# Two joint stretches of small tiles a batch: the next batch's maxima and shifts earlier, the softmax of 96 tokens later, the copies inside the stretch

## The chip, the cores and the metric

One Trainium2 chip, one core of it. The metric is the device time of one execution in microseconds (us); lower is better. The core's engines run side by side, each through its own instructions in order: TensorE (PE) multiplies matrices, VectorE (DVE), ScalarE (ACT) and GpSimd (POOL) work on tiles, and SyncE (SP) starts the transfers (DMA). An instruction waits on semaphores for what it needs, and everything behind it on its engine waits with it.

## The reference

For each of 8 batches and 8 heads (576 tokens, 64 channels, 32 memory slots), and then one feed-forward network over all tokens:

```python
a = exp(phi - max over tokens); a = a / (sum over tokens + 1e-9)
k_m, v_m = a^T k, a^T v                          # 32 slots a head
scores = q k_m^T / 8                             # 32 scores a token
attn = softmax(scores); x = attn v_m             # heads side by side: 512 channels
h = x @ w_in                                     # 512 -> 2048
g = where(h > 0, h, exp(min(h, 0)) - 1)
out = g @ w_out                                  # 2048 -> 512
```

## The kernel before

All matrix products of the network are made three times over: each operand is split into a high part (rounded by an ACT copy) and a low part (what a DVE subtraction leaves), and the products high by high, low by high and high by low are summed. `vw` (the slots' values times `w_in`) is small, so x is never formed: `hidden` multiplies the probabilities `A` by `vw`.

A batch's main loop has 32 iterations, numbered on through the batches: first half of the tokens (288) with 16 blocks j of 128 hidden channels, then the second half. Iteration `it` is a chain over the engines: `hidden(it)` on PE (L812, 6 matmuls into a `psh` bank, of which there are two), `elu_exp` on ACT (L827, L828), `elu_max` and `elu_rest` on DVE (L839, L847), `elu_high` on ACT (L859), `elu_low` on DVE (L865), and `project(it)` on PE (L873, 6 matmuls into two `pso` banks that gather a half's output). Of a half's 288 tokens 256 go through `project`; the last 32 are kept in `rest`, and after every second batch `rest_project` takes them together (48 matmuls more).

What a batch needs before its loop is made while the previous batch's loop runs:

- summaries: `load_phi`, `phi_max` (DVE, L442: the maximum over tokens, `nm`), `spread_max` (two DMAs on SP: L278 writes `nm` to DRAM as `nmd`, L281 reads it back into all rows as `nmb`), `load_e`, `e_shift` (POOL, L286: adds `nmb` to a second copy `e` of phi that lies by token), `e_exp` (ACT, L290), `phi_exp` (ACT, L447, gives the sums), `slot_scale`, and `slots` (PE, L493: the sums k_m and v_m)
- scores: 192 tokens are one score group `u`; `turn` (DVE, L641) transposes it, `softmax_max`, `softmax_shift`, `softmax_exp`, `softmax_sum`, `softmax_divide` (L654, L675, L679, L685 to L688, L696) and `turn_back` (L718) follow, and `probs_high`, `probs_low` (L740, L754) split the result into `A`
- `vw` for four blocks `c` of 512 hidden channels (L566), with `vw_high` (ACT, L768) and `vw_low` (DVE, L774).

Small tiles on PE (`vw`, scores, `slots`: 64 rows by 32 columns) stand together in two stretches a batch from batch 3 on. The first, 10.1 iterations before the batch's loop, holds `vw` of c = 1 and 0 and the scores of two groups; the second, 2.9 iterations into it, holds `vw` of c = 2 and 3, the next batch's `slots` and the third score group.

The order is a hand-written list `FIRST` up to the start of batch 2's loop, and from there a plan: `at(place, step)` gives each step a number in iterations (`base` is the batch's first iteration), the steps are sorted by it, and each engine gets its instructions in that order. SP's queue gets its transfers in the same order. By rule `hidden(it)` has place it - 1.7, `elu_high` it - 1, `project` it + 0.6; an `it` in the set `behind` has its `hidden` at it - 1.35, which puts a `project` between a stretch and it. Banks are named by letters: w, x, y, z are the four `pso` banks, h the two `psh`, b the two `psb`. Tiles of 2 KB a row come from one pool of seven buffers (`t2k`).

Of the kernel before, what the change touches and what calls it, by code (L numbers as in the profile page):

```python
# [8 lines left out]
F32 = mybir.dt.float32  # L9
# [165 lines left out]
def fused_kernel(ctx: ExitStack, tc: tile.TileContext, phiT, phi, kv0, kvt, kv, kvb, q0, q1, w_in, w_out, out):  # L175
# [64 lines left out]
    def units(b):  # L240

        if b < NB:
            return (0, HALF), (HALF, S)
        return (0, 192), (192, 384), (384, 576)
# [29 lines left out]
    def spread_max(b):  # L274

        s = st[b]
        d = dram.tile([2, P], F32, name="nmd")
        nc.sync.dma_start(d.rearrange("a x -> x a"), s["nm"])  # L278
        s["nmb"] = work.tile([P, 2 * P], F32, name="nmb", bufs=1)[:, :P]
        for a in range(2):  # L280
            nc.sync.dma_start(s["nmb"][64 * a : 64 * a + 64], d[a].partition_broadcast(64))  # L281
# [153 lines left out]
    def phi_max(b, g=None):  # L435
# [6 lines left out]
        eng.tensor_reduce(s["nm"][:, g], s["ph"][:, g], AX.X, ALU.max, negate=True)  # L442

# [167 lines left out]
    def scores_part(b, u, outs):  # L611
        by_head(outs, st[b]["kvm"][:, 0], st[b]["q"][u])
        st[b]["ps"]["s", u] = outs

    def scores_first(b):
        ps = [bank([P, 2, UT], "b") for _ in range(2)]
# [3 lines left out]
    def next_slots(b):  # L620
# [3 lines left out]
        if b + 1 == B:  # L624
            return
# [6 lines left out]
    def scores_last(b):  # L632
        scores_part(b, 2, [x[:, :UT] for x in st[b].pop("both")])

    def turn(b, u):

        s = st[b]
        n = s["q"][u].shape[-1]
        sc = temp(b, "sc", u, 2 * n)
        for a, ps in enumerate(s["ps"].pop(("s", u))):  # L640
            nc.vector.transpose(sc[:, a * n : (a + 1) * n], ps)  # L641
        s["sc"][u] = sc.rearrange("p (n m) -> p n m", m=SQ)

    def softmax_max(b, u):
# [6 lines left out]
        else:  # L651
            sc = st[b]["sc"][u]
            mx = mx[:, : sc.shape[1]]
# [3 lines left out]
    def softmax_shift(b, u):  # L657
# [15 lines left out]
        n = sc.shape[1]  # L673
        eng = nc.gpsimd if (b, u) in shift_on_pool else nc.vector
        eng.tensor_tensor(sc, sc, mx.unsqueeze(2).to_broadcast([P, n, SQ]), ALU.subtract)  # L675
# [5 lines left out]
    def softmax_sum(b, u):  # L681
        sc = st[b]["sc"][u]
        n = sc.shape[1]
        sm = work.tile([P, 2 * HALF // SQ], F32, name="sm")[:, :n]
        nc.vector.tensor_reduce(sm, sc, AX.X, ALU.add)  # L685
        nc.vector.tensor_scalar(sm, sm, EPS, None, ALU.add)
        rs = work.tile([P, 2 * HALF // SQ], F32, name="rs")[:, :n]
# [331 lines left out]
    def summaries(b, o, phi_at, max_at, e_at, kv_at, exp_at, shift_at, e_exp_at):  # L1019
        at(o + phi_at, load_phi, b)  # L1020
# [130 lines left out]
```

## Time and profile before

| | |
|---|---|
| median of 3 runs | 728.88 us (728.75 to 730.68) |
| the profiled execution's own time, and its span | 732.18 us, 730.3 us |
| PE busy in the span | 700.3 us (96%) |
| DVE, ACT, POOL busy | 458.2, 455.8, 66.3 us (63%, 62%, 9%) |
| mean granted TensorE clock | 0.992 of full speed |

The span is what the trace covers; the time has 1.9 us more around it. The profiled execution was 3.3 us (0.45%) above the median, so terms are summed against its own time and the result is then carried to the median. A busy PE in this profile is not PE at its peak: matmuls that begin late can be shown as busy.

### The profile page before, as it was taken

The page shows a single profiled execution, that of the slowest core. Times are in us where ns is not written, and L with a number is a line of the kernel's source. Part 1 is how long each engine was busy: PE and PEld are TensorE (multiplying, and loading weights), DVE is VectorE, ACT ScalarE, POOL GpSimd, SP SyncE. Part 2 cuts the span into 40 slices and gives each one's busy share as a digit, 9 for nine tenths or more (in the row PEclk, how much of TensorE's full clock was granted, in tenths as well). Part 3 has the DMA queues.
Part 4 walks back from the last instruction along what each step waited for, and adds up shares of the span by engine and source line. Part 5 has one row for each costly group of instructions (what it writes and reads, how often), then busy time and mean ns, then how long its engine had stood idle before and what let it go on. Part 6 is the DMA issues. An engine that isn't in the chain of part 4 may idle for free.

```text
span 730.3 us, 14339 instructions
## 1 busy us (share of the span) xinstructions
PE 700.3 (96%) x5496; PEld 582.3 (80%) x5496; DVE 458.2 (63%) x1207; ACT 455.8 (62%) x1101; POOL 66.3 (9%) x111
## 2 busy tenths in 40 slices
PE   7899999997999998999989999899989999999997
PEld 7778888886878877788867888678878787878886
DVE  3989888974586358464663646755584554856442
ACT  2879988875357556666653665656565555656652
POOL 0322342122000101000000000100010000000000
PEclk9999999999999999999999999999999999999999
DMA  9972023330302514201222011310141200000001
GB/s 345 408 310 87 2 90 109 115 121 19 131 34 77 198 62 167 83 13 62 75 92 78 32 62 43 154 66 1 62 167 37 73 1 30 1 30 0 30 1 44
DMA packets 25780, 64.14 MB, mean 88 GB/s; under 512 B 4848, under 2 KB 6384, under 8 KB 25712
## 3 DMA queue, kind: packets, MB, share of 16 engines
q1 hardware_dynamic: 25040, 63.06, 24.1%
q8 instruction: 44, 0.72, 0.4%
q10 hardware_dynamic: 672, 0.16, 0.1%
q14 instruction: 24, 0.20, 0.1%
HBM read 53.77 MB, written 9.44 MB: 87 GB/s over the span
## 4 chain that ended last, share of the span: by engine, by line
PE 75%; DVE 11%; ACT 5%; DMA 5%; issue 3%; POOL 1%; SPq 0%; POOLq 0%; DVEq 0%; ACTq 0%
PE pso L873 44%; PE psh L812 22%; DMA nmd<-nm 2%; PE psb L493 2%; DVE gf L839 2%; PE psb L566 2%; PE pso L566 2%; DVE vw L774 2%; ACT gf L828 1%; PE psh L566 1%; DMA nmb<-nmd 1%; ACT gf L827 1%; ACT gp L859 1%; DVE gp L865 1%; DMA kvt<-kv 1%
## 5 line engine op out<-in xcount | busy, mean ns | idle before, releaser
L873 PE MATMUL pso<-wout,gp 128*128 128x512 f32 x1728 | 441.7, 395 | 13.2 <-DVE gp L865 8.7
L873 PEld LDWEIGHTS pso<-wout,gp 128*128 128x128 f32 x1728 | 310.9, 189 | 75.7 <-DVE gp L865 11.1
L812 PEld LDWEIGHTS psh<-A,vw 128*128 128x128 f32 x1536 | 226.2, 188 | 37.1 <-issue 5.5
L812 PE MATMUL psh<-A,vw 128*128 128x288 f32 x1536 | 245.3, 297 | 7.0 <-DVE vw L774 3.4
L859 ACT CAST gp<-gf 128x256 fp32r<-128x256 f32 x256 | 103.3, 405 | 94.2 <-DVE gf L839 83.2
L827 ACT ACTIVATE gf<-psh 128x288 f32<-128x288 f32 x256 | 104.4, 408 | 84.0 <-PE psh L812 79.8
L865 DVE TENSOR_TENSOR gp<-gf,gp 128x256 fp32r<-128x256 f32 x256 | 112.3, 441 | 67.4 <-ACT gp L859 67.0
L839 DVE SCALAR_TENSOR_TENSOR gf<-gf,psh 128x256 f32<-128x256 f32 x192 | 80.1, 417 | 114.3 <-ACT gf L828 112.2
L828 ACT ACTIVATE gf<-gf 128x288 f32<-128x288 f32 x256 | 113.9, 445 | 8.1
L286 POOL TENSOR_TENSOR e<-e,nmb 128x512 f32<-128x512 f32 (+1 forms) x18 | 19.1, 1082 | 334.7 <-DMA e<-phi 155.4
L836 DVE SCALAR_TENSOR_TENSOR gf<-gf,psh 128x288 f32<-128x288 f32 x64 | 28.5, 450 | 17.5 <-ACT gf L828 16.3
L847 DVE SCALAR_TENSOR_TENSOR rest<-gf,psh 128x32 f32<-128x32 f32 x192 | 34.5, 180 | 0.0
L774 DVE TENSOR_TENSOR vw<-psh,vw 128x512 fp32r<-128x512 f32 x20 | 12.9, 686 | 24.4 <-ACT vw L768 24.4
L917 ACT CAST gp<-rest 128x256 fp32r<-128x256 f32 x32 | 12.6, 405 | 21.9 <-PE pso L873 21.9
L768 ACT CAST vw<-psh 128x512 fp32r<-128x512 f32 x20 | 10.8, 589 | 23.8 <-PE psh L566 23.8
L855 POOL COPY rest<-gf 128x32 f32<-128x32 f32 x64 | 18.6, 317 | 71.3 <-DVE gf L836 71.3
L922 DVE TENSOR_TENSOR gp<-rest,gp 128x256 fp32r<-128x256 f32 x32 | 12.9, 420 | 15.6 <-ACT gp L917 15.6
L388 ACT ACTIVATE mag<-raw 128x512 uint32<-128x512 uint32 x30 | 20.1, 672 | 2.7 <-DVE win L410 1.4
L384 ACT ACTIVATE mag<-raw 128x512 f32<-128x512 f32 x30 | 19.6, 666 | 0.0
L774 DVE TENSOR_TENSOR vw<-pso,vw 128x512 fp32r<-128x512 f32 (+1 forms) x28 | 17.4, 629 | 2.5 <-ACT vw L768 2.0
L493 PEld LDWEIGHTS psb<-kvt,e 64*32 64x32 f32 x864 | 13.6, 111 | 3.4 <-issue 3.3
L970 PE MATMUL pso<-ident 128*128 128x128 f32 x84 | 13.6, 325 | 1.6 <-POOL ident masks.py:199 1.6
(137 smaller groups left out, 482.1 us busy)
## 6 DMA issues: line engine op xcount, KB each, us to landing
kvt<-kvb SPq DMA_DIRECT2D x24, 512.0 KB, 6.4
raw<-w_in SPq DMA_DIRECT2D x15, 512.0 KB, 8.0
raw<-w_out SPq DMA_DIRECT2D x15, 512.0 KB, 8.2
out<-osb SPq DMA_DIRECT2D x14, 512.0 KB, 2.8
qt<-q SPq DMA_DIRECT2D x18, 384.0 KB, 4.5
kvt<-kv SPq DMA_DIRECT2D x8, 512.0 KB, 9.5
ph<-phiT SPq DMA_DIRECT2D x7, 576.0 KB, 5.0
e<-phi SPq DMA_DIRECT2D x12, 256.0 KB, 4.6
```

What stands on the lines that cost most here:

```text
L493: nc.tensor.matmul(ps[a][32 * j : 32 * j + 32], e[r, 32 * j : 32 * j + 32], t[r, k % 2, :, j], start=(k == 0), stop=(k == NBL - 1), tile_p ...
L566: nc.tensor.matmul(outs[a][32 * j : 32 * j + 32, :], lhs[r, 32 * j : 32 * j + 32], rhs[r, j], start=True, stop=True, tile_position=(64 * a ...
L774: nc.vector.tensor_tensor(t[:, LO, a, n0:n1], s["ps"]["vw", c, n0][a], t[:, HI, a, n0:n1], ALU.subtract)
L812: nc.tensor.matmul(ps, t[:, x, g, c0 : c0 + P], s["A"][hf][:, y, g, :], start=(n == 0), stop=(n == 5),)
L827: nc.scalar.activation(gf, ps, AF.Relu, scale=-1.0)
L828: nc.scalar.activation(gf, gf, AF.Exp, scale=-1.0)
L836: nc.vector.scalar_tensor_tensor(gf, gf, -1.0, ps, ALU.add, ALU.max)
L839: nc.vector.scalar_tensor_tensor(gf[:, :n], gf[:, :n], -1.0, ps[:, :n], ALU.add, ALU.max)
L847: nc.vector.scalar_tensor_tensor(rest_of(b, j)[:, o : o + REST], gf[:, n:], -1.0, ps[:, n:], ALU.add, ALU.max)
L859: nc.scalar.copy(gp[:, HI], gs[it][:, : NT * P])
L865: eng.tensor_tensor(gp[:, LO], gf[:, : NT * P], gp[:, HI], ALU.subtract)
L873: nc.tensor.matmul(ps, gp[:, y], wout[j][:, x, :], start=(first and n == 0), stop=(last and n == 2),)
```

## The change

`spread_max` no longer writes 256 single numbers: `phi_max` now also copies the two maxima of each row 16 times over into a 32-column tile (L453) and transposes that in 32 by 32 blocks on DVE (L454), so that 8 rows hold 32 numbers each, and the write to DRAM (L282) takes these 8 rows. This holds for batches 2 to 7. Places of the summaries move: `load_phi` from -14 to -21, `phi_max` from -11.3 to -18, `load_e` from -8.5 to -17, `phi_exp` from -6.45 to -16.2, `e_shift` from -5 to -14, `e_exp` from -3.3 to -13 (all against the running batch's base). The second score group of batches 3 to 7 is cut into two softmax units of 96 tokens, and the one that belongs to the second half of the tokens is worked on after the loop's start. In the first stretch `vw` of c = 1 and the scores change banks, and all four copies of a stretch's two `vw` blocks stand directly behind it. `base + 5` joins `behind`. The last batch's second stretch has another order.

```diff
     def spread_max(b):
 
         s = st[b]
-        d = dram.tile([2, P], F32, name="nmd")
-        nc.sync.dma_start(d.rearrange("a x -> x a"), s["nm"])
-        s["nmb"] = work.tile([P, 2 * P], F32, name="nmb", bufs=1)[:, :P]
+        t = s["nmb"]
+        nT = t[:, P + SQ : P + 2 * SQ]
+        d = dram.tile([2, P // SQ, SQ], F32, name="nmd")
+        nc.sync.dma_start(d.rearrange("a r x -> r a x"), nT[:: SQ // 2])
+        s["nmb"] = t[:, :P]
...
         eng.tensor_reduce(s["nm"][:, g], s["ph"][:, g], AX.X, ALU.max, negate=True)
+        if b >= NB:
+            s["nmb"] = t = work.tile([P, 2 * P], F32, name="nmb", bufs=1)
+            n = t[:, P : P + SQ].rearrange("p (a x) -> p a x", a=2)
+            nc.vector.tensor_copy(n, s["nm"].unsqueeze(2).to_broadcast([P, 2, SQ // 2]))
+            nc.vector.transpose(t[:, P + SQ : P + 2 * SQ], t[:, P : P + SQ])
...
     def turn(b, u):
...
+        if b > NB:
+            sc = sc.rearrange("p (a n m) -> p a n m", a=2, m=SQ)
+            if u == 1:
+                s["sc"][1], s["sc"][2] = sc[:, :, :3], sc[:, :, 3:]
+            else:
+                s["sc"][u] = sc
+            return
...
+        if b > NB:
+            if u != 2:
+                s["pr_of"] = t2k([P, 2, UT], "pr")
+            t = s["pr_of"]
+            if u in (1, 2):
+                t = t[:, :, (u - 1) * 96 : u * 96]
+                for a in range(2):
+                    nc.vector.transpose(t[:, a], sc[:, a].rearrange("p n m -> p (n m)"))
...
     def copies(b, c, *places):
         for a, x in enumerate(places):
             at(x, vw_high, b, c, 0, CW, (a,))
-            at(x + 0.01, vw_low, b, c, 0, CW, (a,))
+            at(x, vw_low, b, c, 0, CW, (a,))
...
     for b in range(3, B):
         base = 2 * NJ * b
         o = base - 10.1
-        at(o, vw, b, 1, 0, CW, "wx")
+        at(o, vw, b, 1, 0, CW, "bb")
         at(o, vw, b, 0, 0, CW, "hh")
-        at(o, scores_first, b)
-        copies(b, 0, o + 0.01, o + 0.03)
+        at(o, scores_first, b, "wx")
+        for c in (1, 0):
+            copies(b, c, o, o)
         softmax(b, 0, base - 9.2, 0, 1, 2, 3, 4, 5)
         softmax(b, 1, base - 7.7, 0, 1, 2, 3, 4, 5)
-        copies(b, 1, base - 6.4, base - 5.4)
         if b + 1 < B:
-            summaries(b + 1, base, -14, -11.3, -8.5, -8.2, -6.45, -5, -3.3)
-            slots_done(b + 1, base, 4.3, 5.4, 6)
+            summaries(b + 1, base, -21, -18, -17, -8.2, -16.2, -14, -13)
+            slots_done(b + 1, base, 4.3, 7.4, 6)
+        softmax(b, 2, base + 1.7, None, 0, 1, 2, 3, 4)
         o = base + 2.9
         at(o, vw, b, 2, 0, CW, "yz")
-        at(o, vw, b, 3, 0, CW, "hh")
-        at(o, next_slots, b)
-        at(o, scores_last, b)
-        copies(b, 3, o + 0.01, o + 0.03)
-        softmax(b, 2, base + 4.2, 0, 1, 2, 3, 4, 5)
-        copies(b, 2, base + 4.4, base + 5.35)
-        behind.add(base - 8)
...
+        copies(b, 2, o, o)
+        if b + 1 == B:
+            at(o, turn, b, 3)
+        copies(b, 3, o, o)
+        softmax(b, 3, base + 5.3, 0 if b + 1 < B else None, 1, 2, 3, 4, 5)
+        behind |= {base - 8, base + 5}
```

Three places in the order of instructions follow. First DVE behind the first stretch of batch 4, before: from the second score group's maximum (L654, `mx<-sc`) over a late copy of `vw` and the first group's sum and division to the next `elu_low` (L865).

```order
L865 TENSOR_TENSOR gp<-gf,gp 128x256
L654 TENSOR_REDUCE mx<-sc 128x12
L675 TENSOR_TENSOR sc<-sc,mx 128x384
L839 SCALAR_TENSOR_TENSOR gf<-gf,psh 128x256
L847 SCALAR_TENSOR_TENSOR rest<-gf,psh 128x32
L774 TENSOR_TENSOR vw<-pso_4371,vw 128x512
L685 TENSOR_REDUCE sm<-sc 128x12
L686 TENSOR_SCALAR sm<-sm 128x12
L688 RECIPROCAL rs<-sm 128x12
L696 TENSOR_TENSOR sc<-sc,rs 128x384
L865 TENSOR_TENSOR gp<-gf,gp 128x256
```

The same place now (the lines are those of the changed kernel: L907 is `elu_low`, L881 and L889 `elu_max` and `elu_rest`).

```order
L907 TENSOR_TENSOR gp<-gf,gp 128x256
L681 TENSOR_REDUCE mx<-sc 128x6
L701 TENSOR_TENSOR sc<-sc,mx 128x2x96
L881 SCALAR_TENSOR_TENSOR gf<-gf,psh 128x256
L889 SCALAR_TENSOR_TENSOR rest<-gf,psh 128x32
L712 TENSOR_REDUCE sm<-sc 128x12
L713 TENSOR_SCALAR sm<-sm 128x12
L715 RECIPROCAL rs<-sm 128x12
L722 TENSOR_TENSOR sc<-sc,rs 128x384
L907 TENSOR_TENSOR gp<-gf,gp 128x256
```

The second group's two steps are half as wide, and the copy `vw<-pso` is gone from between the two `elu_low`; it stands, with the other three, in front of this piece.

Then PE at the second stretch of batch 4, before: `vw` twice, `slots`, scores, and what follows.

```order
L566 MATMUL psh<-win_81,kvm 32x512 x8
L493 MATMUL psb<-kvt,e 32x128 x72
L566 MATMUL psb<-qt,kvm 32x192 x8
L812 MATMUL psh<-A,vw 128x288 x6
L873 MATMUL pso_4793<-wout_781,gp 128x512 x3
L873 MATMUL pso_4794<-wout_781,gp 128x512 x3
L812 MATMUL psh<-A,vw 128x288 x6
```

And now (L854 is `hidden`, L915 `project`).

```order
L578 MATMUL psh<-win_81,kvm 32x512 x8
L505 MATMUL psb<-kvt,e 32x128 x72
L578 MATMUL psb<-qt,kvm 32x192 x8
L915 MATMUL pso_4812<-wout_781,gp 128x512 x3
L915 MATMUL pso_4813<-wout_781,gp 128x512 x3
L854 MATMUL psh<-A,vw 128x288 x12
```

A `project` now stands between the stretch and the two `hidden` whose banks the stretch has used.

Last ACT between the two stretches, some 13 iterations before a loop's start, now (L869 and L870 are `elu_exp`, L901 `elu_high`, L459 `phi_exp`, L297 `e_exp`); before, the rows of L459 and L297 were not here but behind the first stretch.

```order
L945 COPY osb<-pso_3767 128x512
L459 ACTIVATE ph,sums<-ph,nm 128x576
L901 CAST gp<-gf 128x256
L869 ACTIVATE gf<-psh 128x288
L870 ACTIVATE gf<-gf 128x288
L459 ACTIVATE ph,sums<-ph,nm 128x576
L901 CAST gp<-gf 128x256
L869 ACTIVATE gf<-psh 128x288
L870 ACTIVATE gf<-gf 128x288
L901 CAST gp<-gf 128x256
L869 ACTIVATE gf<-psh 128x288
L870 ACTIVATE gf<-gf 128x288
```

Behind these rows follow three times one `e_exp` (L297), one `elu_high` and one `elu_exp`, and then the four copies of the stretch.

## Rows read from the trace of the kernel before

**Rows 1.** The chain of waits in order of time: start us, us, what. Nine iterations.

```profile
329.67 1.39 PE pso L873 x6
...
349.23 1.38 PE pso L873 x6
```

**Rows 2.** The chain of waits, ahead of batch 2's `slots`.

```profile
163.97 8.14 DMA nmd<-nm
...
172.69 4.44 DMA nmb<-nmd
...
177.20 1.26 POOL e L286
```

**Rows 3.** Timeline of PE there: start us, us, what, [idle before <-releaser].

```profile
180.84 2.93 PE L873 MATMUL pso<-wout,gp 128*128 128x512 f32 x6 [4.16 <-ACT gp L859]
183.70 3.30 PE L493 MATMUL psb<-kvt,e 64*32 64x128 f32 x144
```

**Rows 4.** Windows: stretch, us; busy of PE, PEld, DVE, ACT, POOL; PEclk; DMA.

```profile
180.00:190.00 10.00, 9.16 (x170) 7.72 (x171) 3.34 (x9) 5.31 (x14) 0.68 (x3) 0.71 0.38 126
```

**Rows 5.** Timelines of ACT and PE ahead of batch 3's `slots`.

```profile
242.33 0.63 ACT L290 ACTIVATE e<-e 128x512 f32<-128x512 f32 x1 [2.78 <-POOL e L286]
...
243.31 1.76 PE L873 MATMUL pso<-wout,gp 128*128 128x512 f32 x6 [0.36 <-ACT gp L859]
...
245.79 2.39 PE L493 MATMUL psb<-kvt,e 64*32 64x128 f32 x144
```

**Rows 6.** Timeline of PE: first stretches of batches 3, 4 and 7.

```profile
269.57 1.09 PE L566 MATMUL pso<-win,kvm 64*32 64x512 f32 x16
...
350.55 1.09 PE L566 MATMUL pso<-win,kvm 64*32 64x512 f32 x16
...
353.07 1.67 PE L873 MATMUL pso<-wout,gp 128*128 128x512 f32 x6
...
616.91 1.09 PE L566 MATMUL pso<-win,kvm 64*32 64x512 f32 x16
```

**Rows 7.** Timeline of PE: second stretch of batch 3, its first and the next row.

```profile
303.88 1.09 PE L566 MATMUL pso<-win,kvm 64*32 64x512 f32 x16
...
308.12 1.06 PE L812 MATMUL psh<-A,vw 128*128 128x288 f32 x6
```

**Rows 8.** Timeline of PE: `rest_project` with one `project`.

```profile
376.66 12.75 PE L873 MATMUL pso<-wout,gp 128*128 128x512 f32 x54
```

**Rows 9.** Timeline of PE: waits of batch 4, and one of batch 7.

```profile
364.83 0.62 PE L873 MATMUL pso<-wout,gp 128*128 128x512 f32 x2
367.26 1.19 PE L873 MATMUL pso<-wout,gp 128*128 128x512 f32 x4 [1.81 <-DVE gp L865]
...
371.13 1.04 PE L812 MATMUL psh<-A,vw 128*128 128x288 f32 x6 [0.50 <-DVE sums L454]
...
408.48 0.66 PE L812 MATMUL psh<-A,vw 128*128 128x288 f32 x3 [0.47 <-DVE vw L774]
...
652.69 1.06 PE L812 MATMUL psh<-A,vw 128*128 128x288 f32 x6 [1.08 <-DVE vw L774]
```

**Rows 10.** Timelines of SP, POOL and DVE behind batch 4's first stretch.

```profile
358.02 1.09 SPq L281 DMA_DIRECT2D nmb<-nmd  x2
...
363.67 3.25 POOL L286 TENSOR_TENSOR e<-e,nmb 128x512 f32<-128x512 f32 x3 [77.51 <-DMA e<-phi]
...
363.44 0.69 DVE L774 TENSOR_TENSOR vw<-pso,vw 128x512 fp32r<-128x512 f32 x1
...
365.29 1.32 DVE L696 TENSOR_TENSOR sc<-sc,rs 128x384 f32<-128x384 f32 x1
...
370.00 0.56 DVE L696 TENSOR_TENSOR sc<-sc,rs 128x384 f32<-128x384 f32 x1
```

**Rows 11.** Small transfers: chain of waits; DMA issues (KB, us to landing).

```profile
0.73 2.85 DMA touch<-kv
...
out<-orest SPq DMA_DIRECT2D x14, 64.0 KB, 1.7
```

More of the change, by code (lines that the diff above doesn't have):

```diff
@@ L243, in units @@
             return (0, HALF), (HALF, S)
[L244 removed]
+        if b == NB:
+            return (0, 192), (192, 384), (384, 576)
+        return (0, 192), (192, 288), (288, 384), (384, 576)
     def bank(shape, where):
@@ L612, in scores_part, with keep, scores_first @@
         by_head(outs, st[b]["kvm"][:, 0], st[b]["q"][u])
-        st[b]["ps"]["s", u] = outs
-    def scores_first(b):
-        ps = [bank([P, 2, UT], "b") for _ in range(2)]
+        st[b]["ps"]["s", (0, 1, 3)[u]] = outs
+    def keep(b):
+        st[b]["kept"] = t2k([P, 2 * UT], "sc")
+    def scores_first(b, where):
+        ps = [bank([P, 2, UT], x) for x in where]
         for u in range(2):
@@ L632, in scores_last, with per_block @@
     def scores_last(b):
-        scores_part(b, 2, [x[:, :UT] for x in st[b].pop("both")])
+        both = st[b].pop("both", None) or [bank([P, UT], "h") for _ in range(2)]
+        scores_part(b, 2, [x[:, :UT] for x in both])
     def turn(b, u):
         s = st[b]
-        n = s["q"][u].shape[-1]
-        sc = temp(b, "sc", u, 2 * n)
+        n = UT
+        sc = s.pop("kept") if u == 0 and "kept" in s else temp(b, "sc", u, 2 * n)
         for a, ps in enumerate(s["ps"].pop(("s", u))):
             nc.vector.transpose(sc[:, a * n : (a + 1) * n], ps)
+        if b > NB:
[5 more added lines that the diff above has]
+            return
         s["sc"][u] = sc.rearrange("p (n m) -> p n m", m=SQ)
+    def per_block(t, sc):
+        if len(sc.shape) == 3:
+            return t[:, : sc.shape[1]]
+        return t[:, : 2 * sc.shape[2]].rearrange("p (a n) -> p a n", a=2)
     def softmax_max(b, u):
@@ L652, in softmax_max @@
             sc = st[b]["sc"][u]
-            mx = mx[:, : sc.shape[1]]
+            mx = per_block(mx, sc)
             nc.vector.tensor_reduce(mx, sc, AX.X, ALU.max)
@@ L682, in softmax_sum @@
         sc = st[b]["sc"][u]
-        n = sc.shape[1]
-        sm = work.tile([P, 2 * HALF // SQ], F32, name="sm")[:, :n]
+        sm = per_block(work.tile([P, 2 * HALF // SQ], F32, name="sm"), sc)
         nc.vector.tensor_reduce(sm, sc, AX.X, ALU.add)
         nc.vector.tensor_scalar(sm, sm, EPS, None, ALU.add)
-        rs = work.tile([P, 2 * HALF // SQ], F32, name="rs")[:, :n]
+        rs = per_block(work.tile([P, 2 * HALF // SQ], F32, name="rs"), sc)
         nc.vector.reciprocal(rs, sm)
@@ L715, in turn_back @@
             s["pr", u] = pr.rearrange("p (g s) -> p g s", g=2)
+            return
+        if b > NB:
[6 more added lines that the diff above has]
+                    nc.vector.transpose(t[:, a], sc[:, a].rearrange("p n m -> p (n m)"))
+            else:
+                nc.vector.transpose(
+                    t.rearrange("p a x -> p (a x)"), sc.rearrange("p a n m -> p (a n m)")
+                )
+            s["pr", u] = t
             return
@@ L1002, in softmax @@
     def softmax(b, u, o, *steps):
-        turned, shifted, exped, divided, back, parts = (o + x for x in steps)
-        at(turned, turn, b, u)
+        shifted, exped, divided, back, parts = (o + x for x in steps[1:])
+        if steps[0] is not None:
+            at(o + steps[0], turn, b, u)
         at(shifted, softmax_max, b, u)
```

26 lines of the change are left out of this document (19 added, 7 removed).

## The prediction, on record before the run

> **What bounds the kernel now.** I read the page's busy shares first: PE is busy 700.3 of 730.3 us, so PE's order and its pauses set the end, and the other engines matter only where PE waits for them. The chain of waits, read in order of time, is a ladder of `project` and `hidden` with few other rungs; nine undisturbed iterations take 349.23 - 329.67 = 19.56 us, 2.173 us each [rows 1]. I then looked for the places that are longer than their iterations, in PE's timeline and the windows. There are three kinds.
>
> The first is one place ahead of batch 2's `slots`. The DMA that writes `nm` to DRAM takes 8.14 us, the read back 4.44, then POOL shifts `e` [rows 2]. ACT's queue holds an `e_exp` in front of an `elu_high`, and PE waits 4.16 us for that `elu_high` [rows 3]. Behind the pause PE is slow: the granted clock of the next window is 0.71, a mixture of the levels 1.2 and 2.4 GHz [rows 4], six `project` matmuls take 2.93 us where an undisturbed six takes 1.38 [rows 1, 3], and `slots` 3.30 where batch 3's takes 2.39 [rows 3, 5].
>
> The second is the same chain in batch 3, where ACT waits 2.78 us for POOL, and PE only 0.36 [rows 5]. That also tells how much slack the chain ACT to PE has: 2.78 - 0.36 = 2.4 us.
>
> The third is in every batch from 3 on. Between the first stretches of batches 3 and 7 lie 616.91 - 269.57 = 347.3 us, four batches [rows 6]. Their work, at the pace of undisturbed rows: 128 iterations of 2.173 are 278.1; four first stretches of 353.07 - 350.55 = 2.52 are 10.1 [rows 6]; four second ones of 308.12 - 303.88 = 4.24 are 17.0 [rows 7]; `rest_project` comes twice, 48 of 54 matmuls in 12.75, so 22.7 [rows 8]. That is 327.9, and 19.4 are lost, 4.9 a batch. Batch 4 shows the three waits that hold most of it: 1.81 and 0.50 behind the first stretch, 0.47 behind the second [rows 9]. The row before the first wait ends early and is cut in two (364.83 to 367.26 for two matmuls), so about 0.2 a wait is lost beside what is shown as idle. Batch 7 has the small two alike and 1.08 at its second stretch [rows 9].
>
> Why PE waits 1.81 is seen on DVE: between two `elu_low` it does the second group's maximum and shift, a late `vw` copy of 0.69, and the first group's sum and division, and the division takes 1.32 us, where 4.7 us later the same operation takes 0.56 [rows 10]. The difference is POOL's `e_shift`, which runs from 363.67 for 3.25 us [rows 10].
>
> **The change part by part.** The write of `nmd`: 256 runs of one number become 8 runs of 32. No row shows that shape. From below it is bounded by 1.7 us (stores of `orest`, 32 runs), from above by the 8.14 of now; 128 short runs (`touch`) take 2.85 [rows 2, 11]. I take 2.3, between the two nearest. Added on DVE are a copy and a transpose of 32 columns; I allow 0.4 for both (bounds 0.2 and 0.8, the latter more than the 0.56 of a 384-wide operation [rows 10]). The shift of `e` can so begin 8.14 - 2.3 - 0.4 = 5.4 us earlier. PE's pause there was 4.16, so it closes, with about 0.2 left because PE next waits for what ACT does by itself. Without the pause I expect no drop of the clock: 2.93 - 1.38 = 1.55 and 3.30 - 2.39 = 0.91 come back. Sum: 4.16 + 1.55 + 0.91 - 0.3 = 6.3 (bounds 4.0 and 6.6). By the Trainium skill ("DMA: Bandwidth & Descriptors", the section on the increment by 16), a transfer whose outermost dimension is 4 is spread over at most four engines; the new write has 4 outermost, which speaks against so short a time. No row here shows such a transfer; were it as slow as a quarter of the engines could make the old one, the write would not shrink at all, which is the last rival below.
>
> Batch 3's wait: 0.36 and some slow start, 0.5 (bounds 0 and 0.7).
>
> Behind the first stretch: taken away between the two `elu_low` are the `vw` copy (0.69), half of the second group's two steps (about 0.28 each, half of the 0.56 of such a width), and POOL's disturbance (1.32 - 0.56 = 0.76) [rows 10]. That is 2.0 us, against a wait of 1.81 with 0.2 beside it: the wait closes. What is late next is the following `elu_max`, behind the division; it has the first group's `turn_back` and a half-wide sum and division after it instead of full ones, so I find it in time by some tenths. The 0.50 wait came from the same queue two iterations later, in which `slot_scale` and another full sum and division stood; it closes too.
>
> The copies go into the stretch. ACT and DVE have nothing to do while PE makes small tiles: the four ACT copies and four DVE subtractions (0.69 each [rows 10]) begin when the first block is done, about 1 us into the stretch, and end about 4.1 us after its start. Queued behind them is one `elu_low`, so 4.5; PE, after 2.5 us of stretch, one `project` (1.4) and two `hidden` (1.6), wants it at 5.5. Cover gone, each missing 0.1 us is paid by PE in ten places. At the second stretch `hidden` needed a bank or a `vw` part that was late (0.47, and 1.08 in batch 7); now a `project` of 1.4 us lies between, and c = 2 is copied before its iterations.
>
> Moved work: `phi_exp`, `e_shift` and `e_exp` go where DVE and ACT idle in each iteration. The stiffest place is the first `e_exp`, five iterations after `phi_max` (10.9 us; I take off 1.9, most of an iteration, because `phi_max` ends late in its own and `e_exp` stands early in its: 9.0). It needs DVE's 0.4, the write's 2.3, 363.67 - 358.02 = 5.65 from the read's issue to POOL's start, with `e` loaded behind it on SP, and a first shift of about 1.26 [rows 2, 10]: 9.6. ACT waits 0.6, inside the 2.4 of slack. The Trainium skill ("GPSIMD Engine Reference", "Specifications") says that POOL shares its SBUF interface with DVE instructions that have two SBUF inputs; the trace agrees with 1.32 against 0.56. By that rule the disturbance is only moved, to `elu_low`; I put that at nothing, since it would take some tenths of the same slack.
>
> Sum for this kind: of 4.9 a batch, 2.8 is plain waiting and about 0.7 the slow starts beside it; the remaining 1.4 I leave, as PE's entering and leaving of the stretches. 3.5 in four batches are 14.0 (bounds 1.8 and 4.4 each: 7 to 18). Batch 7: 1.08 + 0.50 + 0.47, 2.0 (bounds 1 and 2.6).
>
> **Sum.** 6.3 + 0.5 + 14.0 + 2.0 = 22.8. The profiled execution of 732.18 would be 709.4. It lies 3.3 above the median of the runs; the median of 728.88 becomes 706.1, and I say 706.0.
>
> **The rivals.** One: the forecast, 702 to 712, chance 0.68.
>
> Two: batch 2's pause closes only in part, because another load or ACT's queue ends at nearly the same time. For it: PE is released by ACT there, not by the DMA [rows 3]. Against: the chain of waits runs through the DMA and POOL [rows 2]. Half of the term gone: 709 to 710; with all of it gone, 712. Chance 0.08.
>
> Three: the stretches keep their cost. Copies behind each other and a fuller queue bring new waits in place of the old, so that only 1.8 a batch and 1 in batch 7 come back: 6.3 + 0.5 + 7.2 + 1.0 = 15.0, so 714. For it: the covers above are of 0.2 to 1 us. Against: all covers were added up from full widths. Chance 0.13.
>
> Four: the work moved forward is felt there. ACT gets two `phi_exp` and three `e_exp`, and if `elu_high` is late by 1 us more than its slack twice a batch, 4 batches give back 8: 714. With more, 722. Chance 0.05.
>
> Five, the other side: the write of `nmd` stays at 8.14. Then batch 2 gains nothing and loses 0.4; the first `e_exp` is ready at 9.6 + 5.8 = 15.4 instead of 9.0, ACT waits 6.4, PE 6.4 - 2.4 = 4.0 in four batches, 16 us; and if the clock falls after each as in [rows 3, 4], 2.5 more each, 10. Against 16.0 gained at the stretches that is 10 to 11 slower: 739. It decides from a write of about 6.5 us on. Against it: 8 runs instead of 256. Chance 0.06.
>
> **How the numbers follow.** 706.0 is the likeliest case. 702 to 713 holds one and two; three and four lie just above it and five far, so about 2 in 10 are left out. A change under 0.3% (2.2 us) could not be told from none. Faster takes cases one to four but for 0.02 of the last, 0.91; slower case five and small mishaps, 0.06; same 0.03.
>
> **What would show it.** The issue of `nmd` to its landing near 2.3 us, and PE without the 4.16 and with a granted clock near 1 at 170 to 190. Behind a first stretch no wait of PE for `elu_low`, and a division that is nowhere 1.32. From first stretch to first stretch about 77.5 us, and 11.3 more where `rest_project` lies between. I am wrong if `e_exp` waits more than 2.4 us for POOL, or if PE waits behind the stretches for copies of `vw` or for `elu_low`.

## The result and the profile after

The changed kernel takes 702.58 us (median of 6 runs, 702.2 to 703.36), the kernel before 728.82 (6 runs, 728.35 to 730.8): a ratio of 0.9634 with an interval of 0.962 to 0.9649, or 26.2 us less. Forecast were 706.0 and a range of 702 to 713.

The page of the changed kernel, section 1 (busy time, share of the span, instructions), the line of the chain that ended last, and two groups of section 5 (busy us, mean ns | idle before):

```profile
PE 691.5 (99%) x5496; PEld 580.5 (83%) x5496; DVE 463.3 (66%) x1264; ACT 452.2 (65%) x1106; POOL 66.5 (9%) x111
...
PE 94%; DMA 4%; DVE 0%; ACT 0%; issue 0%; SPq 0%
...
L915 PE MATMUL pso<-wout,gp 128*128 128x512 f32 x1728 | 439.3, 394 | 0.1
...
L854 PE MATMUL psh<-A,vw 128*128 128x288 f32 x1536 | 241.5, 295 | 0.7 <-ACT A L777 0.4
```

PE idles 9.2 us of 700.7, in the opening and behind its last products. Ahead of `project` and `hidden` 0.8 us of idle time are left. Ahead of batch 2's `slots`, where [rows 3] have a pause of 4.16, the timeline of PE has none, and the windows give the granted clock (third from the end of the row) as 1.00 where [rows 4] have 0.71:

```profile
173.22 1.74 PE L854 MATMUL psh<-A,vw 128*128 128x288 f32 x12
174.80 1.53 PE L915 MATMUL pso<-wout,gp 128*128 128x512 f32 x6
176.26 2.25 PE L505 MATMUL psb<-kvt,e 64*32 64x128 f32 x144
178.44 1.06 PE L854 MATMUL psh<-A,vw 128*128 128x288 f32 x6
```

```profile
170.00:180.00 10.00, 10.00 (x192) 8.82 (x191) 6.00 (x15) 6.40 (x17) 3.25 (x7) 1.00 0.21 55
180.00:190.00 10.00, 10.00 (x94) 8.34 (x94) 6.21 (x15) 4.60 (x13) 1.44 (x7) 1.00 0.51 186
```

The cause is in SP's queue. The trace has no landing for the new write, but SP issues the read back only when the write is over, and that is 164.41 - 162.72 = 1.69 us behind the write's issue, where the old write took 8.14 [rows 2]. SP's timeline ahead of batch 2's `slots`:

```profile
162.72 0.67 SPq L282 DMA_DIRECT2D nmd<-nmb  x1
164.41 1.15 SPq L285 DMA_DIRECT2D nmb<-nmd  x2
```

For the other batches it is 1.66 to 1.72 us, once 2.24. The reads back have the same shape as before and are faster too. The views of their lines give the time to landing, before (L281) and now (L285):

```profile
DMA to landing us min/median/max: 3.6/4.3/4.8
...
DMA to landing us min/median/max: 2.4/2.4/2.5
```

The first stretches in PE's timeline, to be laid beside [rows 6]:

```profile
260.19 1.09 PE L578 MATMUL psb<-win,kvm 64*32 64x512 f32 x16
...
337.09 1.09 PE L578 MATMUL psb<-win,kvm 64*32 64x512 f32 x16
...
590.92 1.09 PE L578 MATMUL psb<-win,kvm 64*32 64x512 f32 x16
```

From batch 3's to batch 7's it is 330.73 us, 16.6 less than the 347.34 before. Behind them DVE's timeline (batch 4) shows all four `vw` subtractions done at 341.3, the `elu_low` that was queued behind them starting 4.15 us after the stretch began, and the first group's division at 0.56, where [rows 10] have 1.32:

```profile
338.84 1.29 DVE L816 TENSOR_TENSOR vw<-psb,vw 128x512 fp32r<-128x512 f32 x2 [1.59 <-ACT vw L810]
340.04 1.28 DVE L816 TENSOR_TENSOR vw<-psh,vw 128x512 fp32r<-128x512 f32 x2
341.24 0.42 DVE L907 TENSOR_TENSOR gp<-gf,gp 128x256 fp32r<-128x256 f32 x1
...
350.45 0.56 DVE L722 TENSOR_TENSOR sc<-sc,rs 128x384 f32<-128x384 f32 x1
```

### The profile page after: what moved, and what is told of

Same layout as the page of the kernel before. It is cut to its first block, busy times and chain, and to the rows that moved or that the text cites. A ratio compares the mean times of both kernels' runs of the same rounds, so it can differ in the third digit from the quotient of the medians.

```text
span 700.7 us, 14399 instructions
## 1 busy us (share of the span) xinstructions
PE 691.5 (99%) x5496; PEld 580.5 (83%) x5496; DVE 463.3 (66%) x1264; ACT 452.2 (65%) x1106; POOL 66.5 (9%) x111
## 4 chain that ended last, share of the span: by engine, by line
PE 94%; DMA 4%; DVE 0%; ACT 0%; issue 0%; SPq 0%
PE pso L915 57%; PE psh L854 29%; PE psb L578 3%; PE psb L505 2%; DMA raw<-w_out 2%; PE pso L578 2%; DMA raw<-w_in 1%; PE psh L578 1%; DMA qh<-q 1%; DMA ph<-phiT 0%; PE psb L591 0%; PE pso L591 0%; PE psb L547 0%; PE psh L734 0%; DVE A L791 0%
## 5 line engine op out<-in xcount | busy, mean ns | idle before, releaser
L915 PE MATMUL pso<-wout,gp 128*128 128x512 f32 x1728 | 439.3, 394 | 0.1
L915 PEld LDWEIGHTS pso<-wout,gp 128*128 128x128 f32 x1728 | 310.2, 188 | 62.5 <-issue 4.9
L854 PEld LDWEIGHTS psh<-A,vw 128*128 128x128 f32 x1536 | 226.3, 188 | 25.1 <-DVE gp L907 2.5
L854 PE MATMUL psh<-A,vw 128*128 128x288 f32 x1536 | 241.5, 295 | 0.7 <-ACT A L777 0.4
L901 ACT CAST gp<-gf 128x256 fp32r<-128x256 f32 x256 | 103.5, 405 | 99.4 <-DVE gf L881 89.2
L907 DVE TENSOR_TENSOR gp<-gf,gp 128x256 fp32r<-128x256 f32 x256 | 114.7, 450 | 59.2 <-ACT gp L901 57.7
L869 ACT ACTIVATE gf<-psh 128x288 f32<-128x288 f32 x256 | 104.5, 408 | 70.0 <-PE psh L854 66.9
L881 DVE SCALAR_TENSOR_TENSOR gf<-gf,psh 128x256 f32<-128x256 f32 x192 | 80.1, 417 | 99.4 <-ACT gf L870 99.2
L870 ACT ACTIVATE gf<-gf 128x288 f32<-128x288 f32 x256 | 113.9, 445 | 8.1
L878 DVE SCALAR_TENSOR_TENSOR gf<-gf,psh 128x288 f32<-128x288 f32 x64 | 28.5, 450 | 17.1 <-ACT gf L870 15.4
L889 DVE SCALAR_TENSOR_TENSOR rest<-gf,psh 128x32 f32<-128x32 f32 x192 | 34.5, 180 | 0.0
L816 DVE TENSOR_TENSOR vw<-psb,vw 128x512 fp32r<-128x512 f32 (+2 forms) x40 | 20.9, 561 | 10.5 <-ACT vw L810 10.5
L810 ACT CAST vw<-psb 128x512 fp32r<-128x512 f32 (+2 forms) x40 | 17.6, 488 | 8.1 <-PE psb L578 8.0
L578 PE MATMUL psb<-win,kvm 64*32 64x512 f32 (+2 forms) x320 | 17.9, 504 | 0.0
L816 DVE TENSOR_TENSOR vw<-pso,vw 128x512 fp32r<-128x512 f32 (+1 forms) x18 | 10.1, 598 | 10.0 <-ACT vw L810 9.9
```

The costliest lines, as they stand in the source:

```text
L578: nc.tensor.matmul(outs[a][32 * j : 32 * j + 32, :], lhs[r, 32 * j : 32 * j + 32], rhs[r, j], start=True, stop=True, tile_position=(64 * a ...
L816: nc.vector.tensor_tensor(t[:, LO, a, n0:n1], s["ps"]["vw", c, n0][a], t[:, HI, a, n0:n1], ALU.subtract)
L854: nc.tensor.matmul(ps, t[:, x, g, c0 : c0 + P], s["A"][hf][:, y, g, :], start=(n == 0), stop=(n == 5),)
L869: nc.scalar.activation(gf, ps, AF.Relu, scale=-1.0)
L870: nc.scalar.activation(gf, gf, AF.Exp, scale=-1.0)
L878: nc.vector.scalar_tensor_tensor(gf, gf, -1.0, ps, ALU.add, ALU.max)
```

## The experiments

In the runs of the experiments the kernel before took about 736 us and not 729 (735.71, 735.78 and 736.22 in three sets), and the changed one 702.59. Every experiment is therefore set against these. The start of the first stretch of batch 3, the way to that of batch 7 and the rest, from each profile (the three add up to the span). The execution that was profiled lies within 1 us of the median, but for the first profile of before (3.3 above its median) and e6 (2.4 above):

| kernel | median us | to batch 3 | 3 to 7 | 7 to end |
|---|---|---|---|---|
| before, first profile | 728.82 | 269.57 | 347.34 | 113.39 |
| e0 before, again | 735.71 | 269.28 | 351.27 | 113.35 |
| e1 new write alone | 720.32 | 260.65 | 345.02 | 113.33 |
| e10 new write and copies | 709.22 | 260.63 | 335.76 | 111.31 |
| e4 changed | 702.59 | 260.00 | 330.49 | 109.81 |
| e3 late summaries | 703.48 | 260.04 | 331.39 | 109.77 |
| e5 no split | 704.69 | 260.78 | 331.60 | 110.12 |
| e7 order | 704.40 | 260.77 | 330.62 | 111.01 |
| e8 c = 1 late | 706.60 | 260.68 | 333.46 | 110.46 |
| e9 no split, c = 2 late | 711.43 | 260.57 | 337.63 | 111.30 |
| e6 c = 1 and 2 late | 718.01 | 261.56 | 345.26 | 111.68 |
| e2 old write | 741.25 | 280.45 | 350.16 | 109.79 |

**e0, the kernel before again, and e4, the changed kernel again.** No edit.

> The kernel before once more, unchanged, for a second profile. The first profile stands 3.3 us above the median of its runs, and its part ahead of batch 2, which the change leaves alone, took 1.7 us more than in the profile of the changed kernel. Theory: the 3.3 us lie in that opening part and in the tail, and the waits behind the stretches of batches 3 to 6 come again as they were (2.8 to 3.3 us of shown idle in each batch). Rival: the waits behind the stretches vary from execution to execution by 0.5 us or more a batch, so that part of the 16.6 us between the first stretches of batches 3 and 7 is a chance of that one profile.

> The changed kernel itself, unchanged, as the measure for the runs beside it: times between chips differ (the kernel before had 728.8 in one set of runs and 735.7 in another). Theory: the changed kernel hardly depends on how long the write of the maxima takes, so its time is 702.6 again within 1 us even where the kernel before is slower. Rival: it moves with the kernel before, to 707 to 709 where that takes 735.

The second profile of before has a span of 733.9 and an `e0` time of 735.8. Its opening is shorter (the maximum of batch 2 starts at 161.01, not 162.59), but its waits are longer. PE's timeline:

```profile
242.72 1.75 PE L873 MATMUL pso<-wout,gp 128*128 128x512 f32 x6 [1.83 <-ACT gp L859]
286.83 1.20 PE L873 MATMUL pso<-wout,gp 128*128 128x512 f32 x4 [2.65 <-DVE gp L865]
...
368.29 1.20 PE L873 MATMUL pso<-wout,gp 128*128 128x512 f32 x4 [2.48 <-DVE gp L865]
...
544.63 1.91 PE L873 MATMUL pso<-wout,gp 128*128 128x512 f32 x4 [3.01 <-DVE gp L865]
```

So the waits do vary, 1.83 here against the 0.36 of [rows 5], 2.48 against the 1.81 of [rows 9]. The rival of e0 says more than that: the two profiles come from two sets of runs, and no run shows that the waits vary as much from execution to execution within one set. Batch 4's longer wait has its cause on POOL and DVE. The shift starts 14.2 us behind the start of the stretch and not 13.1, and runs into the `elu_low` that PE waits for, which took 0.67 in the first profile:

```profile
365.15 3.40 POOL L286 TENSOR_TENSOR e<-e,nmb 128x512 f32<-128x512 f32 x3 [78.65 <-DMA e<-phi]
...
366.76 1.48 DVE L865 TENSOR_TENSOR gp<-gf,gp 128x256 fp32r<-128x256 f32 x1
```

The write of `nmd` took 8.5 us in the median here and 8.1 in the first profile, the reads 4.6 and 4.3. The changed kernel does not notice: 702.59 us against 702.58, as the theory of e4 has it.

**e1, the new write alone.** `phi_max` and `spread_max` of the change put into the kernel before:

```
+            nc.vector.tensor_copy(n, s["nm"].unsqueeze(2).to_broadcast([P, 2, SQ // 2]))
+            nc.vector.transpose(t[:, P + SQ : P + 2 * SQ], t[:, P : P + SQ])
...
-        nc.sync.dma_start(d.rearrange("a x -> x a"), s["nm"])
+        nc.sync.dma_start(d.rearrange("a r x -> r a x"), nT[:: SQ // 2])
```

> The kernel before with one part of the change: the new way of spreading the maxima (copy, transpose, 8 runs of 32 numbers). Theory: the pause and the slow clock ahead of batch 2's summaries go, and batch 3's wait, 6.3 + 0.5 = 6.8 us or a little more; behind the first stretches the shift on POOL comes some 5 us earlier and no longer meets the division, so the wait of 1.8 to 2.3 us there falls by up to 0.76 in four batches, 0 to 3 us. Together 7 to 10 us less than before, 719 to 722. Rival (the second of the prediction): another load or ACT's own queue holds PE there, and only half of the pause closes: 3 to 4 us less, 725. A third: all of the change's gain is this part, 703.

720.32 us, 15.4 less than before in the same runs (ratio 0.979, 0.9759 to 0.9821). Ahead of batch 3's stretch 8.6 us are gained against e0, and PE has no wait there, so the prediction's rival two falls. The other 6.25 lie between batches 3 and 7, but against the first profile of before it is only 2.3, so most of it is time that the kernel before loses in these runs alone. Behind the first stretches the first wait is still 0.90 to 1.09, against 1.81 to 2.32 in the first profile and 2.48 to 3.01 in e0, and the wait of 0.5 two iterations later is unchanged. POOL, DVE and PE in batch 4:

```profile
347.96 3.55 POOL L291 TENSOR_TENSOR e<-e,nmb 128x512 f32<-128x512 f32 x3 [77.23 <-ACT gp L869]
...
349.69 1.50 DVE L685 TENSOR_TENSOR sc<-sc,mx 128x384 f32<-128x384 f32 x1
351.12 0.68 DVE L875 TENSOR_TENSOR gp<-gf,gp 128x256 fp32r<-128x256 f32 x1
...
357.76 1.20 PE L883 MATMUL pso<-wout,gp 128*128 128x512 f32 x4 [1.06 <-DVE gp L875]
361.63 1.03 PE L822 MATMUL psh<-A,vw 128*128 128x288 f32 x6 [0.50 <-DVE sums L464]
```

POOL's shift now comes 6.9 us behind the stretch's start (341.04) and not 13.1 as in [rows 6, 10], and meets another operation of DVE: the first group's shift takes 1.50, the second's, undisturbed, 0.56. The disturbance has moved and not gone.

**e2, the old write in the changed kernel.** The edit of e1 the other way round, everything else as changed.

> The changed kernel with the old way of spreading the maxima (256 runs of one number), everything else as changed. It puts a price on the rival on the slower side. Theory: the write takes 8.1 us again; batch 2's and 3's places lose 7 to 7.7 us; in four batches the first exponential of the summaries waits 5.7 to 7.1 us for POOL, of which 2.4 are slack, so PE waits 3.3 to 4.7 each, 16 in all: 726, and 736 if the clock falls behind each of these waits as it did ahead of batch 2. Rival: the exponential has more slack than I worked out, and only batches 2 and 3 lose: 710.

741.25 us: 38.7 more than the changed kernel, and 0.8% slower than before (ratio 1.0083, 1.0053 to 1.0112). ACT's and PE's timelines ahead of batch 3's first stretch, and the window:

```profile
273.86 0.63 ACT L292 ACTIVATE e<-e 128x512 f32<-128x512 f32 x1 [8.65 <-POOL e L288]
...
274.84 2.93 PE L905 MATMUL pso<-wout,gp 128*128 128x512 f32 x6 [6.21 <-ACT gp L891]
```

```profile
270.00:280.00 10.00, 5.16 (x17) 4.41 (x18) 2.41 (x7) 4.72 (x12) 3.09 (x3) 0.66 0.74 288
```

PE waits 6.21, 3.87, 4.58 and 4.39 in the four batches, and behind three of these waits six `project` matmuls take 2.9 us (behind the other one five take 2.50), with a granted clock of 0.66 in this window, a mixture of 1.2 and 2.4 GHz. It is the mechanism of rival five, worked out as 739 or 10 more than before; it came out at 741, 5.5 more than before in these runs. The slack of 2.4 between ACT and PE [rows 5] comes out again: 8.65 - 6.21 = 2.44. My expectation for this run, 726 to 736, was too low: batch 3's wait alone, taken at under 1 us from [rows 5], was 3.46.

**e3, the summaries late.** In the changed kernel:

```
-            summaries(b + 1, base, -21, -18, -17, -8.2, -16.2, -14, -13)
+            summaries(b + 1, base, -14, -11.3, -8.5, -8.2, -6.45, -5, -3.3)
```

and without `keep`, a step that sets a buffer of the pool aside for the first score group.

> The changed kernel with the next batch's maxima, shifts and exponentials put back to their old places (around and behind the first stretch), new write kept. Theory: DVE's and ACT's queues behind the first stretch get the slot sums and three exponentials again, and the short wait of 0.5 us two iterations behind it returns, perhaps with part of the longer one: 0.5 to 1.5 us a batch, 2 to 6 us more than the changed kernel. Rival: with the short write and the copies inside the stretch the place of this work is indifferent, within 1 us of the changed kernel.

703.48 us, 0.9 more. PE has no shown wait; batches 3 and 4 lose 0.5 and 0.4 us, the others nothing. The rival holds. Moving this work forward, the largest move of the change, is by itself worth almost nothing once the other parts are there. It isn't without contact either. DVE's timeline has an `elu_low` of 1.11 beside POOL's shift, and the next operation, one of whose inputs is PSUM, at its usual 0.41, still beside POOL (343.90 to 347.4):

```profile
344.37 1.11 DVE L907 TENSOR_TENSOR gp<-gf,gp 128x256 fp32r<-128x256 f32 x1
345.40 0.41 DVE L881 SCALAR_TENSOR_TENSOR gf<-gf,psh 128x256 f32<-128x256 f32 x1
```

**e5, no split.** `units(b)` gives three units of 192 for all of these batches, with one `softmax(b, 2, base + 5.3, ...)` for the last:

```
-        return (0, 192), (192, 288), (288, 384), (384, 576)
+        return (0, 192), (192, 384), (384, 576)
...
-        softmax(b, 2, base + 1.7, None, 0, 1, 2, 3, 4)
```

> The changed kernel with the last 384 tokens of a batch in two units of 192 again in place of 96, 96 and 192; copies and summaries as changed. DVE's five steps on the second unit get their full width behind the first stretch, each 0.2 to 0.3 us longer. Theory: the covers there are of some tenths only, so a wait of 0.3 to 1 us comes back in each of batches 3 to 7: 1.5 to 5 us more than the changed kernel. Rival: with the copies gone from that place DVE has room, and the time is that of the changed kernel within 0.7 us.

704.69 us, 2.1 more. Of the two profiles' difference 0.8 lie ahead of batch 3, where the edit has no part; 1.1 lie between batches 3 and 7, 0.3 a batch, in iterations of 2.23 to 2.26 for 2.17 without a shown wait, and 0.3 behind. So the split is worth about 1.4, just under the theory's low end of 1.5.

**e6, e8, e9, the copies late.** e6 has both edits, e8 the first, e9 the second on top of e5:

```
-        for c in (1, 0):
-            copies(b, c, o, o)
+        copies(b, 0, o, o)
+        copies(b, 1, base - 6.4, base - 5.4)
...
-        copies(b, 2, o, o)
+        copies(b, 2, base + 4.4, base + 5.35)
```

> The changed kernel with the copies of the second and third quarter of the values' products put back to their old places, one at a time in the iterations behind the two stretches (-6.4, -5.4, +4.4, +5.35); split and summaries as changed. Theory: these are what DVE's queue has too much behind the first stretch, and what is late behind the second; waits of 0.5 to 1.1 us and of 0.5 us come back in each of five batches, 5 to 8 us more than the changed kernel. Rival: the short write and the split are enough, and the place of the copies costs under 1 us.

> The changed kernel with only the second quarter's copies (c = 1) back at -6.4 and -5.4 behind the first stretch; those of c = 2 stay inside the second. In the run with both late, the first stretch of batch 3 lost about 0.6 us in two iterations (2.44 and 2.49 for 2.17) without one shown wait. Theory: 0.6 us in five batches, 3 us more than the changed kernel, 705 to 706. Rival: the 15.4 us of the run with both come from the first stretch after all, 712 or more.

> The changed kernel without the split, and with the third quarter's copies (c = 2) back at +4.4 and +5.35; c = 1 stays inside the first stretch. With the split these copies cost 2.3 us a batch at the product that first needs them. Theory: that price was made by the split's own steps, which stand on ACT and DVE ahead of the late copies; without the split only the wait of the kernel before (0.5 us a batch) is left beside the 2.1 of the missing split: 707 to 709. Rival: the late copies cost 2 us a batch by themselves, 713 to 716.

e6 takes 718.01 us, 15.4 more than the changed kernel and twice what I expected. The place was wrong too: behind the first stretch (e8) it is 4.0 more, 0.7 of it in the opening and then 0.7 a batch, again in longer iterations without a shown wait. The bigger part, 718.01 - 706.60 = 11.4, comes from the copies behind the second stretch. ACT's and PE's timelines of e6 in batch 3:

```profile
302.32 0.57 ACT L810 CAST vw<-pso 128x512 fp32r<-128x512 f32 x1
...
304.69 0.57 ACT L810 CAST vw<-pso 128x512 fp32r<-128x512 f32 x1
...
305.31 0.53 PE L854 MATMUL psh<-A,vw 128*128 128x288 f32 x2 [1.03 <-ACT vw L810]
306.53 0.66 PE L854 MATMUL psh<-A,vw 128*128 128x288 f32 x3 [0.68 <-DVE vw L816]
```

The first `hidden` with this quarter comes while ACT and then DVE still copy: 1.71 us in four batches, against 0.47 in [rows 9]; twice the clock fell behind it (granted 0.83 in the windows 475 to 485 and 570 to 580; batches 5 and 6 lost 3.8 us there, batch 3 lost 2.2). Without the split, e9, the copies cost 711.43 - 704.69 = 6.7: neither the theory (707 to 709) nor the rival (713 to 716). So the late copies have a price of their own, about 6.7. The other 4.7 I put down to the split's steps ahead of them in ACT's and DVE's queues, since the first quarter's copies lie some 30 us earlier; but no run had the split with c = 2 alone late, so this part is argued and not shown.

**e7, the order behind the second stretch.**

```
-        behind |= {base - 8, base + 5}
+        behind.add(base - 8)
```

> The changed kernel without the one entry that lets a projection go ahead of the first hidden product behind the second stretch. Theory: that hidden product then needs a bank or a copy that is not there yet, and PE waits about 0.5 us in each of five batches, as the kernel before did at that place: 2 to 3 us more than the changed kernel. Rival: with the copies inside the stretch the product is in time either way, within 0.7 us.

704.40 us, 1.8 more. In batches 3 to 6 nothing is lost (the rival); in batch 7, where the stretch ends with products of `vw`, `hidden` waits 1.11. The other 0.8 lie ahead of batch 3, where the edit has no part, as in e1, e5 and e8 to e10 (260.6 to 260.8 for 260.0); what makes the opening longer in these I can't say. At the stretch of `vw` that begins at 106.87 in e4, ahead of every place that an edit touches, 0.5 to 0.7 of it is there already in e1, e5, e7, e8 and e10 (107.47 in e7).

**e10, new write and copies, nothing else.** e3, e5 and e7 together.

> The kernel before with two parts of the change alone: the new way of spreading the maxima, and all copies inside the two stretches (with the banks that this needs). No split, summaries at their old places, no projection ahead of the first product behind the second stretch. Theory: the missing parts add up as they stood each by itself, 2.1 + 0.9 + 1.8 = 4.8 us over the changed kernel, 707; the copies are then worth 13 of the 17.7 us between the run with the new spreading alone and the changed kernel. Rival: the parts cover for each other, and without all three the waits behind the first stretch are back: 712 or more.

709.22 us, 6.6 more than the changed kernel: between theory (4.8) and rival. Waits of 0.2 to 0.3 are back behind the first stretches, which none of the three edits alone had brought. Between batches 3 and 7, where the openings have no part, the three cost 0.9 (e3), 1.1 (e5) and 0.1 us (e7) one by one, 2.1 in all, and 5.3 together. From before to changed, in these runs, the chain is 735.71, 720.32 with the write, 709.22 with the copies, 702.59 with the rest: 15.4, 11.1 and 6.6. The step of the copies also has the new banks, the later places of `slots_done` and of the third group's softmax and the last batch's order; no run takes these apart.

**e11, eight rows in one dimension.** The DRAM tile is `[4, 2, 32]`, written as `(r a) x` and read as `d[:, a]`.

> The changed kernel with the maxima written to DRAM as eight rows one behind the other (outermost 8) instead of 4 by 2. Theory, by the rule on the increment by 16 in the Trainium skill (DMA: Bandwidth & Descriptors): 4 outermost use at most four of the engines, 8 use eight, and the write gets shorter than 2.4 us, perhaps 2.0. Rival: at 8 runs of 128 bytes the number of engines does not show, and the write takes 2.4 us again. The kernel's time is that of the changed kernel either way, within 0.5 us.

702.58 us in one run. SP's timeline ahead of batch 2's `slots`, for e11 and then for e4:

```profile
162.50 0.71 SPq L282 DMA_DIRECT2D nmd<-nmb  x1
164.24 1.31 SPq L285 DMA_DIRECT2D nmb<-nmd  x2
...
162.54 0.67 SPq L282 DMA_DIRECT2D nmd<-nmb  x1
164.22 1.14 SPq L285 DMA_DIRECT2D nmb<-nmd  x2
```

From the write's issue to the read's it is 1.70 to 1.74 us in e11 (once 2.04) and 1.65 to 1.69 in e4 (once 2.23). The 2.4 us that theory and rival speak of are the landing of the reads back and not of the write. The rival holds in substance: at this size the outermost dimension does not show.

## Why the prediction was right

The waits that the prediction named closed, and the changed kernel lies in the range, but only 0.6 us inside its lower end: every term came out larger than forecast.

**The pause at batch 2: 6.3 forecast.** From the end of the maximum to the first `hidden` behind `slots` it is 6.8 less. Each step is there: write at most 1.7 (forecast 2.3, with 1.7 as the bound from below), copy and transpose 0.18 + 0.21 (0.4), no pause, clock 1.00. The read back, which I had left at 4.44, fell to 2.4; the sum did not need it, since the pause closes either way. That the write is the cause, and not another load or ACT's queue, e1 and e2 show.

**Batch 3: 0.5.** Measured 0.9.

**Batches 3 to 6: 14.0.** Measured 16.6, so this term was too small, in two ways. I read the waits from batch 4 alone, which has the least of the four: it shows 2.78 of idle time, the others 3.00, 3.30 and 3.03. The first wait in batches 3, 5 and 6 of the first profile, from PE's timeline, is longer than the 1.81 of [rows 9]:

```profile
286.49 1.20 PE L873 MATMUL pso<-wout,gp 128*128 128x512 f32 x4 [2.02 <-DVE gp L865]
...
460.26 1.20 PE L873 MATMUL pso<-wout,gp 128*128 128x512 f32 x4 [2.32 <-DVE gp L865]
...
541.36 1.20 PE L873 MATMUL pso<-wout,gp 128*128 128x512 f32 x4 [2.12 <-DVE gp L865]
```

What makes these waits differ is on DVE, and the prediction read it too small. It charged POOL's shift with the longer division alone, 0.76. Two more operations ahead of the wait are longer than they are elsewhere: `sm` (L686, 0.17 undisturbed) and the `elu_low` that PE waits for (0.42 undisturbed). First profile, us, worked out in ns:

| batch | PE's first wait | `sm` longer by | division longer by | `elu_low` longer by | wait without the three |
|---|---|---|---|---|---|
| 3 | 2.02 | 0.43 | 0.75 | 0.25 | 0.60 |
| 4 | 1.81 | 0.20 | 0.76 | 0.25 | 0.60 |
| 5 | 2.32 | 0.73 | 0.75 | 0.25 | 0.60 |
| 6 | 2.12 | 0.52 | 0.75 | 0.24 | 0.61 |

What is left is the same in all four, so POOL's shift had a share of 1.2 to 1.7 us in these waits. In e0 it is 1.9 to 2.1, with 0.61 left in batches 3 to 5 and 1.07 in batch 6. With the shift at another place (e1) the wait is 0.9 to 1.1, so taking it away gives back a little less than its share.

And of the 4.9 lost a batch I left 1.4 to "PE's entering and leaving of the stretches". Only 0.7 of it stayed (330.73 - 327.9 over four batches). The rest was waiting that no row shows as idle, such as the two iterations of 2.46 and 2.28 us instead of 2.17 behind batch 4's two waits.

**The reasons for these 14.0** need sorting. The waits closed, as worked out. But the prices were off: POOL's share was 1.2 to 1.7 and not 0.76, and halving the second group's two steps saved 0.39 (0.55 and 0.56 to 0.35 and 0.36) and not 0.56. And I added the parts up, which the runs do not bear out. Between batches 3 and 7, undone alone in the changed kernel, c = 1's copies cost 3.0 us, the split 1.1, the place of the summaries 0.9; the last two together with the order cost 5.3 where their sum is 2.1 (e10). That each is covered by slack that the others leave is my explanation; no run shows it by itself. POOL's disturbance did not go: it moved to another operation, as the prediction said, and costs nothing where DVE has room. In the changed kernel, with no wait of PE near it:

```profile
418.09 1.39 DVE L907 TENSOR_TENSOR gp<-gf,gp 128x256 fp32r<-128x256 f32 x1
```

**The copies behind the second stretch** I named with 0.47 a batch. In the changed kernel they are the most sensitive place of all (11.4 with the split, 6.7 without), so the change needed them inside the stretch. Why they are so much dearer there than in the kernel before is not shown; that the other parts fill the queues there is a guess.

**The first `e_exp`: a wait of 0.6 forecast, inside 2.4 of slack.** ACT waited 1.41 at batch 4's and PE not at all; what came last there was the load of `e`, not the maxima.

**Batch 7: 2.0.** Measured 3.6. I added up three waits; a fourth of 0.40 for an `elu_low` stood behind the first stretch, the iterations beside them were longer than shown, as above, and the window 720 to 730 had a clock of 0.93 before, where the last of the changed kernel has 1.00.

The terms that the two profiles show add up to 6.8 + 0.9 + 16.6 + 3.6 = 27.9 against 22.8; 1.7 more is an opening that was longer in the first profile. The medians differ by 26.2, because that profile stood 3.3 above its median.

One sum of the prediction has a slip: cases one to four but for 0.02 are 0.92 and not 0.91.

## What to carry to other kernels

Price a recurring place from all of its occurrences, and from the distance between two marks rather than from shown waits: iterations that are 5 or 10% too long hold waiting that no row shows. Costs behind a common slack don't add up: undo parts both one by one and together before saying which one pays. Where a wait differs from batch to batch, look for the operations ahead of it whose lengths differ by as much. A tiny transfer at the head of a chain is worth reshaping first; here it also decides whether later moves gain or lose (702.6 with the short write, 741 with the long).

## What the hardware showed unexpectedly

The kernel before took 729 us in one set of runs and 736 in the others, with a write of 8.1 and 8.5 us; the changed kernel took 702.6 in both. With the new write in it (e1), 15.4 us went in the slower runs. That the slower write makes the difference between the sets is likely, but no run changed that alone.

Moving the numbers is not what makes the old write long. In the first profile the packets of each of the six old writes (256 for the numbers and 16 more, all of 4 bytes) lie within 0.3 us; those of batch 2 lie between 164.87 and 165.12, and the write lands at 172.11. What fills the 7 us no record shows. What is issued behind it is slower too: the reads back land after 4.3 to 5.1 us (medians) in the three profiles with the old write and after 2.4 to 2.7 in the others, large pieces of `e` after 4.6 to 4.7 and 3.3 to 3.9. e1 and e2 change the write alone and show the same.

POOL's shift does not slow DVE's operations by a factor. An operation with two SBUF inputs that begins while one of the shift's three instructions runs ends a fixed time behind the end of that instruction, and so does `sm`, which has one input. In batch 4 of the first profile the three end at 364.96, 366.20 and 366.92; `sm` ends 0.03 behind the first, the division [rows 10] 0.42 behind the second, `elu_low` 0.28 behind the third. POOL's and DVE's timelines:

```profile
363.67 1.29 POOL L286 TENSOR_TENSOR e<-e,nmb 128x512 f32<-128x512 f32 x1 [77.51 <-DMA e<-phi]
364.93 1.27 POOL L286 TENSOR_TENSOR e<-e,nmb 128x512 f32<-128x512 f32 x1
366.16 0.76 POOL L286 TENSOR_TENSOR e<-e,nmb 128x128 f32<-128x128 f32 x1
...
364.62 0.37 DVE L686 TENSOR_SCALAR sm<-sm 128x12 f32<-128x12 f32 x1
366.54 0.67 DVE L865 TENSOR_TENSOR gp<-gf,gp 128x256 fp32r<-128x256 f32 x1
```

Batches 3, 5 and 6 have the same three distances. Sums and reciprocals, with one input, were not held, and neither was an `elu_low` that began within 0.05 us of the shift's start (0.39 at 347.99 in e1). How long such an operation takes therefore depends on when it begins: `elu_low` took 0.42 undisturbed and up to 1.48, `sm` 0.17 and up to 1.27. Operations with an input in PSUM keep their length (0.41 in e3, 0.69 in [rows 10]). The Trainium skill ("GPSIMD Engine Reference", "Specifications") says that the interface is shared for instructions with two SBUF inputs; the runs agree for these, and add how long one waits.

The Trainium skill's rule on the increment by 16 ("DMA: Bandwidth & Descriptors") would have the new write use at most four engines. The traces fit it if each engine that takes part leaves one packet of 4 bytes: beside its eight of 128 bytes the new write has 4 of these, e11's has 8, and the old write, with 128 outermost, 16 beside its 256. At 8 runs of 128 bytes, 4 or 8 outermost made no difference to the time (1.68 and 1.74 us from issue to the read's issue in batch 2).
